# Two of six up parts regular, the input's sums in one later job, maxima across partitions off GpSimd, the last batch's sums on TensorE

## The chip, the cores and the metric

One core of one Trainium2 chip runs the whole program. The metric is the device time of one execution in microseconds, as a median over runs. TensorE (PE), VectorE (DVE), ScalarE (ACT) and GpSimd (POOL) each work through a queue of their own in program order; SyncE (SP) issues the DMAs. An instruction that waits holds up everything behind it on its engine.

## The reference

Batch 4, sequence 448, model width 768, hidden width 3072, all fp32 (the weights of the two later stages arrive as fp64 bits).

```python
attn = 1 / (1 + exp(-(q @ k.T / 8 - log(448))))        # 12 heads of 64
x = concat_heads(attn @ v)                             # 4 x 448 x 768
u = x + real(fft(fft(x, axis=1), axis=2))
un = (u - mean(u)) / sqrt(var(u) + 1e-6)               # over the 768 features
x2 = u + relu(un @ w_ch1) @ w_ch2                      # 768 -> 3072 -> 768
gate = sigmoid(causal_conv5(x2, conv_w))
out = (gate * (x2 @ w_val)) @ w_out
```

## The kernel before, in words

**Order of the work.** The program is written by a planner at build time: jobs are Python generators on a board, and a model of the engines' times decides in which order their instructions are written. At run time only that order and the waits on data count.

**Stages.** First attention (64-row fp32 matmuls), batch by batch, with the Fourier transforms and the layer norm of earlier batches in between. Then the hidden layer in six parts `g` of 512 columns. A part is an *up* product (`un @ w1[g]`, relu, split into two fp16 halves `h`) for all four batches, and a *down* product (`h @ w2[g]`, added into `acc` by VectorE). Each fp32 product is three fp16 matmuls: high by high, high by low, low by high. A down product of one part is 288 matmuls of 128x448. Last come `value` (`wv`) and `project` (`wo`) with the gate.

**Two kinds of up.** `up` is the regular one: 288 matmuls a part. `quad` is a Strassen scheme over a pair of batches, the two halves of the 768 features and two column blocks: seven products instead of eight, 252 matmuls a part. For it the weights are combined (seven blocks in `load_w1`, with adds on VectorE) and the inputs too: `sums(pair)` makes sums and differences `tb` of `un` on GpSimd, with fp16 roundings on ScalarE, 72 GpSimd instructions for both pairs, and overwrites half of the second batch's `un`. The seven results are put together on VectorE and ScalarE in `combine`. Before, part 0 is regular and parts 1 to 5 are Strassen.

**Weights.** Every weight goes through `convert`: 384 columns at a time are loaded as 64-bit words, turned into fp32 by integer instructions (five on VectorE, one on ScalarE), and their largest magnitude is kept. The first three (`w1[0]`, `w2[0]`, `w1[1]`) go into SBUF; the other 13 matrices (`w2[1]`, `w1[2]`, `w2[2]`, and so on to `wo`) go by `stream` back to DRAM and are read again later (`again`) into the one buffer `wf`, since their scale is known only when the whole matrix has been seen. `factor` makes the scale from the largest magnitude over all partitions. For the early three it goes by `peak`: VectorE writes a diagonal `pd`, TensorE multiplies it with ones, VectorE takes the maximum of each row. For the 13 of the stream it goes by `peak_pool`, a `partition_all_reduce` on GpSimd. `load_w2` scales a down weight in four quarters on ScalarE (`wf`, then the fp16 high half `w`) and makes the low half on GpSimd (for part 0 on VectorE).

**Sums of the norm.** `norm(b)` adds up six tiles of features on VectorE or GpSimd, then one fp32 matmul with ones adds over partitions; for the variance the squares are added in the same way before four small fp32 matmuls.

In the profile all engine instructions carry one line (L218, the recorder of the planner), so they are told apart by the names of their tiles.

Of the kernel before, what the change touches and what calls it, by code (L numbers as in the profile page):

```python
# [8 lines left out]
F32 = mybir.dt.float32  # L9
F32R = mybir.dt.float32r  # L10
F16 = mybir.dt.float16
# [40 lines left out]
S_BY = "DVE"  # L52
NABS = 3
H_BY = "POOL"
T_BY = "POOL", "POOL"
# [6 lines left out]
ABSMAX = bass.bass_isa.ReduceOp.absmax  # L62
# [3 lines left out]
class Clock:  # L66
# [4 lines left out]
    def __init__(self):  # L71
        self.at = dict(PE=0.0, DVE=0.0, ACT=0.0, POOL=0.0, SP=0.0)
        self.cells, self.slots, self.spans, self.bytes = {}, {}, {}, {}
        self.port, self.dma, self.log, self.mode = (0.0, ""), 0.0, [], None
# [69 lines left out]
    def put(self, e, cost, reads, writes, lag=0.06, shared=False, tag=None):  # L144
        need = max([self.ready(e, *reads)] + [self.free(e, a) for a in writes])
        start = max(self.at[e], need)
        if shared and start < self.port[0] and self.port[1] != e:
            cost += 0.8 * min(cost, self.port[0] - start)
        end = start + cost
        if shared:  # L150
            self.port = (end, e)
        self.log.append((e, tag, self.at[e], start, end))
        self.at[e] = end
        self.touch(e, reads, writes, end + lag)
        return end

    def note(self, e, op, a, k):
# [24 lines left out]
        if op == "partition_all_reduce":  # L182
            k = dict(out=a[0], in_=a[1])
# [10 lines left out]
        elif e == "POOL":  # L194
            cost = 1.03 if k.get("op") == ALU.pow else 0.41 if op == "partition_all_reduce" else 0.12 + n * (0.002 if out.dtype == F16 else 0.00224)
# [54 lines left out]
def when(go):  # L250
    return (), (), 0, go
# [89 lines left out]
def body(tc, qd, kd, vd, w1d, w2d, cwd, wvd, wod, cdd, k12d, csd, eyed, out):  # L341
# [83 lines left out]
    def peak_pool(m, nm):  # L425
        yield on("DVE", m)
        t = col(nm + "t")
        V.tensor_reduce(out=t, in_=m, axis=AX.X, op=ALU.max)
        yield on("POOL", t)
        g = col(nm + "g")  # L430
        P.partition_all_reduce(g, t, 128, ABSMAX)
        then = ck.at["POOL"] + 4.0
        yield when(lambda: board.by(then))
        return g

# [82 lines left out]
    def first_f32(src, i, exp, nm):  # L518
# [3 lines left out]
        yield from factor(m, W1N, i, exp, nm, True)  # L522
# [5 lines left out]
    def stream():  # L528
# [3 lines left out]
        for i in range(2):  # L532
            jobs += [(wvd[i], ("wv", i), 12 + i, WV_EXP), (wod[i], ("wo", i), 14 + i, WO_EXP)]
# [15 lines left out]
        def scaling():  # L549
            for j, (last, n, key, i, exp, d) in enumerate(ends):  # L550
                yield when(lambda: done[0] >= last)
                yield from factor(mx[:, j % 2], n, i, exp, key[0], False)
# [36 lines left out]
    def load_w1(g, now=None):  # L589
        if g == 0:  # L590
            t, e, s = yield from first_f32(w1d[0], 0, W1_EXP, "w1")
            w = wp.tile([128, 2 * W1N + 128], F16, tag="w1", bufs=1, name="w1")[:, :2 * W1N].rearrange("p (c n) -> p c n", c=2)
            yield from halves_direct(t, s, w[:, 0], w[:, 1])
            w1_of[0] = w[:, 0].rearrange("p (c k f) -> p c k f", c=8, k=3), w[:, 1].rearrange("p (c k f) -> p c k f", c=8, k=3), e
# [4 lines left out]
        yield when(lambda: g - 1 in upped and len(seen) >= 4 * (g - 1) and w1p.at is not None)  # L599
# [8 lines left out]
        his, lows = [], []  # L608

        def low():  # L610
            for i in range(7):
# [11 lines left out]
        for k, c, o, a, b, need in ((0, 0, None, 0, 0, None), (2, 3, None, 0, 0, None), (1, 1, None, 0, 0, None), (3, 3, ALU.add, 2, 3, 2), (5, 2, ALU.subtract, 0, 2, 2), (4, 0, ALU.subtract, 3, 0, 0), (6, 1, ALU.subtract, 1, 0, 1)):  # L623
# [7 lines left out]
        yield when(lambda: len(lows) == 7)  # L631

    def load_w2(g):
# [7 lines left out]
        yield from (halves_direct if g == 0 else halves_scaled)(t, s, w[:, 0], w[:, 1])  # L641
# [28 lines left out]
    def weights(second):  # L670
# [3 lines left out]
        for nm in ("wv", "wo"):  # L674
            for i in range(2):
                yield from load_half(i, nm)
                if (nm, i) == ("wv", 0):
                    yield when(lambda: ("wo", 1) in kept)
# [4 lines left out]
                    for h in range(2):  # L683
# [3 lines left out]
                        r = col(f"evo{h}")  # L687
                        V.tensor_tensor(out=r, in0=em, in1=factors[:, 0, 14 + h:15 + h], op=ALU.mult)
                        evo.append(r)
# [327 lines left out]
    def norm(b):  # L1017
# [5 lines left out]
        e = yield on(SUM_BY, x[:, 0:2], cost=0.6)  # L1023
        ENG[e].tensor_tensor(out=t, in0=x[:, 0], in1=x[:, 1], op=ALU.add)
        e = yield on(SUM_BY, x[:, 2], t, cost=0.6)
        ENG[e].tensor_tensor(out=t, in0=t, in1=x[:, 2], op=ALU.add)
        yield when(lambda: b in mixed)
        for j in (3, 4, 5):
            e = yield on(SUM_BY, t, x[:, j])
            ENG[e].tensor_tensor(out=t, in0=t, in1=x[:, j], op=ALU.add)  # L1030
        yield on("PE", t, go=banks(1))
        mean = ps_m()
        T.matmul(mean[:, :S], ones, t, start=True, stop=True)
# [22 lines left out]
        yield when(lambda: "s0" in sqs)  # L1056
        e = yield on(SUM_BY, tt[:, 0:2])
        ENG[e].tensor_tensor(out=tt[:, 1], in0=tt[:, 1], in1=tt[:, 0], op=ALU.add)
        yield when(lambda: "s1" in sqs)
        e = yield on(SUM_BY, tt[:, 2:4])  # L1060
        ENG[e].tensor_tensor(out=tt[:, 3], in0=tt[:, 3], in1=tt[:, 2], op=ALU.add)
        e = yield on(SUM_BY, tt[:, 1], tt[:, 3])
        ENG[e].tensor_tensor(out=tt[:, 3], in0=tt[:, 3], in1=tt[:, 1], op=ALU.add)
        sqs.append("a")
        yield when(lambda: "s2" in sqs)
        e = yield on(SUM_BY, tt[:, 0:2])
        ENG[e].tensor_tensor(out=tt[:, 1], in0=tt[:, 1], in1=tt[:, 0], op=ALU.add)
        e = yield on(SUM_BY, tt[:, 1], tt[:, 3])
        ENG[e].tensor_tensor(out=tt[:, 1], in0=tt[:, 1], in1=tt[:, 3], op=ALU.add)
        t = tt[:, 1]  # L1070
        yield on("PE", t, go=banks(1))
        var = ps_m()
        for i in range(4):
            T.matmul(var[:CK, i:i + 1], t[:, i * CK:(i + 1) * CK], ones[:, 0:1], start=True, stop=True)
# [44 lines left out]
    def sums(pair):  # L1119
        b, c = 2 * pair, 2 * pair + 1  # L1120
        yield when(lambda: c in normed and ux.at is not None and (pair == 0 or pair - 1 in tb))
        yield when(lambda: ("up", c) in upped)
        w = ux.tile([128, 3, 2, 3, S], F16, name=f"tb{pair}")
        tmp = ux.tile([128, 3, S], F32, tag="tmp", bufs=1, name="tmp")
        x, y, z = (tmp[:, i] for i in range(3))

        def two(out, p, q, op):
            e = yield on(T_BY[pair], p, q)
# [7 lines left out]
        for k in range(3):  # L1136
            yield from two(x, un_hi[b][:, k], un_lo[b][:, k], ALU.add)
            yield from two(y, un_hi[c][:, k], un_lo[c][:, k], ALU.add)
            yield from two(z, un_hi[c][:, k + 3], un_lo[c][:, k + 3], ALU.add)
            yield from two(x, y, x, ALU.subtract)  # L1140
            yield from two(y, z, y, ALU.subtract)
            yield from part(x, w[:, 0, 0, k], w[:, 0, 1, k])
            yield from two(z, z, x, ALU.subtract)
            yield from part(y, un_hi[c][:, k], un_lo[c][:, k])
            yield from part(z, w[:, 1, 0, k], w[:, 1, 1, k])
            yield from two(x, un_hi[b][:, k + 3], un_lo[b][:, k + 3], ALU.add)
            yield from two(x, x, z, ALU.subtract)
            yield from part(x, w[:, 2, 0, k], w[:, 2, 1, k])
        low, high = slice(0, 3), slice(3, 6)
        tb[pair] = [(un_hi[b][:, low], un_lo[b][:, low]), (un_hi[b][:, high], un_lo[b][:, high]), (un_hi[c][:, high], un_lo[c][:, high])]  # L1150
        tb[pair] += [(w[:, 2, 0], w[:, 2, 1]), (w[:, 0, 0], w[:, 0, 1]), (w[:, 1, 0], w[:, 1, 1]), (un_hi[c][:, low], un_lo[c][:, low])]
# [11 lines left out]
    for pair in range(2):  # L1163
        board.add(T_RANK, sums(pair))
# [35 lines left out]
    SLOT = (0, 2), (3, 1)  # L1200

    def up(b):
        pair, o = divmod(b, 2)
        w1h, w1l, _ = w1_of[0]
        for q in range(2):
# [4 lines left out]
            for i in range(2):  # L1210
                m = 0
                for k in range(NT):
                    c = 4 * (i ^ o) + 2 * (k // 3) + q
                    pump()
                    for w, u in ((w1h, un_hi[b]), (w1h, un_lo[b]), (w1l, un_hi[b])):
                        T.matmul(p[:, i, :S], w[:, c, k % 3], u[:, k], start=(m == 0), stop=(m == 17))
# [3 lines left out]
        upped.add(("up", b))  # L1220
# [159 lines left out]
    ups, downs = list(range(B)), list(range(B))  # L1380
    force(lambda: 0 in w1_of)
    while downs:
        if ups:
            can_down = 0 in w2_of and downs[0] not in ups
            force(lambda: ups[0] in normed or 0 in w2_of and downs[0] not in ups)
            if ups[0] in normed:
                up(ups.pop(0))
                if not ups:
                    upped.add(0)
                continue  # L1390
        force(lambda: 0 in w2_of)
        down(0, downs.pop(0))
    downed.add(0)
# [29 lines left out]
    def value(b, j):  # L1423
        force(lambda: b in xs_of and ("wv", j // 3) in halves)
# [19 lines left out]
    def project(b, j):  # L1444
        force(lambda: ("wo", j // 3) in halves)
# [120 lines left out]
```

## Time and profile before

| | us |
|---|---|
| median of 3 runs | 1063.74 (1062.57 to 1064.6) |
| the profiled execution | 1060.32 |
| its span, first to last instruction | 1058.5 |
| TensorE busy in the span | 995.3 (94%) |
| VectorE busy | 796.2 (75%) |
| ScalarE busy | 490.3 (46%) |
| GpSimd busy | 317.0 (30%) |

Busy times of TensorE count matmuls that overlap; how much the stage needs is better read from the distance between starts. The page's 40 slices show TensorE at 9 tenths or more nearly everywhere; slices 14 to 16 (344 to 423 us) show 5 tenths, and there its granted clock falls to 8, 8 and 7 tenths.

### The profile page before, as it was taken

To read this page: it belongs to the slowest core of one execution; us is meant where nothing else is said; L and a number is where in the kernel's file an instruction comes from. 1 tells how busy PE (TensorE), PEld (TensorE's weight loads), DVE (VectorE), ACT (ScalarE), POOL (GpSimd) and SP (SyncE) were. 2 spreads that over 40 slices of the span, in tenths; PEclk is the share of its full clock that TensorE was granted. 3 is DMA by queue.
4 is the path that set the end of the run, shared out by engine and by line. 5 is a ranking of instruction groups with operands and counts; after the bars stand their busy time and mean duration, and the time that the engine had idled before them with its cause. 6 is when DMAs were issued, how large, how long until landed. Compare 5 with 4: busy or idle time off the path is not lost.

```text
span 1058.5 us, 15662 instructions
## 1 busy us (share of the span) xinstructions
PE 995.3 (94%) x5913; PEld 514.4 (49%) x5913; DVE 796.2 (75%) x1498; ACT 490.3 (46%) x691; POOL 317.0 (30%) x231
## 2 busy tenths in 40 slices
PE   9899999999989555999999989997999999999998
PEld 4344544664545222555555545543555555555554
DVE  4868988879999944887989879957983477776530
ACT  6786756243244344234623452433433588434321
POOL 0104333327959832013302330033113565000000
PEclk9999999999999887999999999999999999999999
DMA  7752340010222443276435544643441021010001
GB/s 235 215 164 82 118 142 1 3 40 22 62 67 90 134 149 115 73 233 198 143 127 178 173 135 150 180 149 109 132 157 46 1 90 46 1 44 36 28 34 70
DMA packets 54547, 110.29 MB, mean 104 GB/s; under 512 B 6456, under 2 KB 30408, under 8 KB 54472
## 3 DMA queue, kind: packets, MB, share of 16 engines
q1 hardware_dynamic: 54472, 109.30, 32.3%
q8 instruction: 46, 0.75, 0.3%
q14 instruction: 29, 0.24, 0.1%
HBM read 84.76 MB, written 24.38 MB: 103 GB/s over the span
## 4 chain that ended last, share of the span: by engine, by line
PE 72%; DVE 17%; issue 6%; ACT 2%; POOL 2%; DMA 1%; SPq 0%; DVEq 0%; POOLq 0%; ACTq 0%
PE ps_m L218 58%; PE ps_s L218 14%; DVE wabs L218 6%; DVE wf L218 3%; DVE c L218 2%; DVE acc L218 1%; DVE tt L218 1%; DVE pm L218 1%; POOL tt L218 1%; POOL w L218 1%; DMA w<-wod 1%; POOL h L218 1%; ACT c L218 0%; DMA v<-vd 0%; SPq L218 0%
## 5 line engine op out<-in xcount | busy, mean ns | idle before, releaser
L218 PE MATMUL ps_m<-h,w 128*128 128x448 f16 x1728 | 332.9, 355 | 14.2 <-POOL w L218 10.2
L218 PEld LDWEIGHTS <-w 128*128 128x128 f16 x2016 | 198.3, 99 | 201.8 <-issue 11.0
L218 ACT ACTIVATE wabs<-w 128x384 f32<-128x384 f32 (+1 forms) x119 | 65.1, 550 | 155.8 <-DMA w<-w2d 44.9
L218 DVE SCALAR_TENSOR_TENSOR wabs<-w,wabs 128x384 int32<-128x384 int32 x192 | 130.7, 681 | 4.7
L218 PEld LDWEIGHTS <-w1hi 128*128 128x128 f16 x840 | 82.9, 99 | 97.7 <-issue 22.0
L218 DVE SCALAR_TENSOR_TENSOR acc<-ps_m,rg,acc 128x448 f32<-128x448 f32 x144 | 97.9, 680 | 38.8 <-PE ps_m L218 36.4
L218 POOL TENSOR_TENSOR h<-c,h 128x896 f16<-128x896 f32 x40 | 77.9, 1952 | 102.5 <-ACT h L218 66.8
L218 ACT ACTIVATE sg<-ps_s,logb 128x896 f32<-128x896 f32 x84 | 83.6, 1004 | 32.1 <-PE ps_s L218 31.2
L218 ACT ACTIVATE c<-c 128x896 f32<-128x896 f32 x40 | 38.0, 950 | 121.6 <-DVE c L218 119.8
L218 PE MATMUL ps_m<-sg,v 64*64 64x448 f32 x672 | 84.1, 548 | 3.6 <-DVE zl L218 2.6
L218 PE MATMUL ps_s<-q,k 64*64 64x448 f32 x672 | 83.5, 543 | 4.2 <-ACT sg L218 4.2
L218 PE MATMUL ps_m<-xs,wv 128*128 128x448 f16 x432 | 84.6, 352 | 0.0
L218 PE MATMUL ps_m<-gh,wo 128*128 128x448 f16 x288 | 80.8, 352 | 0.0
L218 PE MATMUL ps_s<-tb,w1hi 128*128 128x448 f16 x240 | 65.3, 353 | 13.6 <-POOL tb L218 10.7
L218 DVE SCALAR_TENSOR_TENSOR gp<-acc,cw,gp 128x448 f32<-128x448 f32 x84 | 61.4, 731 | 21.8 <-ACT gp L218 19.9
L218 DVE TENSOR_SCALAR_CACHE_REDUCE wabs<-wabs 128x384 f32<-128x384 f32 x120 | 65.3, 544 | 7.4 <-ACT wabs L218 7.1
L218 PE MATMUL ps_s<-un,w1hi 128*128 128x448 f16 x240 | 67.1, 362 | 0.2 <-DVE c L218 0.2
L218 PEld LDWEIGHTS <-w1lo 128*128 128x128 f16 x420 | 41.5, 99 | 51.9 <-issue 14.4
L218 PE MATMUL ps_m<-un,w1hi 128*128 128x448 f16 x240 | 65.0, 352 | 0.0
L218 PEld LDWEIGHTS <-wo 128*128 128x128 f16 x432 | 42.3, 98 | 39.5
L218 PEld LDWEIGHTS <-wv 128*128 128x128 f16 x432 | 42.1, 98 | 39.2
L218 PE MATMUL ps_s<-un,w 128*128 128x448 f16 x288 | 57.7, 360 | 0.0
(170 smaller groups left out, 1512.2 us busy)
## 6 DMA issues: line engine op xcount, KB each, us to landing
w<-w1d SPq DMA_DIRECT2D x48, 384.0 KB
w<-w2d SPq DMA_DIRECT2D x48, 384.0 KB
w<-wabs SPq DMA_DIRECT2D x72, 192.0 KB
wf<-w SPq DMA_DIRECT2D x36, 384.0 KB
q<-qd SPq DMA_DIRECT2D x24, 224.0 KB
out<-o SPq DMA_DIRECT2D x24, 224.0 KB
k<-kd SPq DMA_DIRECT2D x23, 224.0 KB
w<-wvd SPq DMA_DIRECT2D x12, 384.0 KB
```

The costliest lines, as they stand in the source:

```text
L218: return f(*a, **k)
```

## The change

Five edits. (1) `REG = 2`: parts 0 and 1 are regular, 2 to 5 Strassen; `load_w1(1)` makes four blocks and no sums of weights. (2) `sums` is one job for both pairs. It starts when the last batch is normed and `w2[0]` is made, keeps `un` whole, and makes the one operand that overwrites `un` only after the regular part 1 has read it; 84 GpSimd instructions in place of 72. (3) Every maximum across partitions goes by `peak`; `peak_pool` is gone. (4) For the last batch (`BY_PE`) the sums of mean and variance are accumulated by TensorE from the single tiles: 6 fp32 matmuls for 1, and 24 small ones for 4. (5) `w2[0]` is split as the later ones (low half on GpSimd); `wv` and `wo` stream in the order wv, wv, wo, wo; the planner's model of the port that VectorE and GpSimd share is another.

```diff
-T_BY = "POOL", "POOL"
+REG = 2
+START = 0
+T_BY = "POOL"
+BY_PE = (3,)
...
-    def factor(m, n, i, exp, nm, early):
-        g = yield from (peak if early else peak_pool)(m[:, :n // COLS], nm)
+    def factor(m, n, i, exp, nm):
+        g = yield from peak(m[:, :n // COLS], nm)
...
 def load_w1(g, now=None):
-        yield when(lambda: g - 1 in upped and len(seen) >= 4 * (g - 1) and w1p.at is not None)
+        yield when(lambda: g - 1 in upped and len(seen) >= 4 * (g - REG) and w1p.at is not None)
+        num = 4 if g < REG else 7
+        plan = [(0, 0, None, 0, 0, None), (1, 1, None, 0, 0, None), (3, 2, None, 0, 0, None), (2, 3, None, 0, 0, None)]
...
 def load_w2(g):
-        yield from (halves_direct if g == 0 else halves_scaled)(t, s, w[:, 0], w[:, 1])
+        yield from halves_scaled(t, s, w[:, 0], w[:, 1])
...
 def norm(b):
+        if b in BY_PE:
+            mean = ps_m()
+            for j in range(NT):
+                if j == 2:
+                    yield when(lambda: b in mixed)
+                yield on("PE", x[:, j])
+                T.matmul(mean[:, :S], ones, x[:, j], start=(j == 0), stop=(j == NT - 1))
...
+            for k in range(3):
+                yield when(lambda: f"s{k}" in sqs)
+                for h in range(2):
+                    q = tt[:, 2 * k % 4 + h]
+                    for i in range(4):
+                        T.matmul(var[:CK, i:i + 1], q[:, i * CK:(i + 1) * CK], ones[:, 0:1], start=(k + h + i == 0), stop=(k + h + i == 6))
...
-    def sums(pair):
-        yield when(lambda: c in normed and ux.at is not None and (pair == 0 or pair - 1 in tb))
-        yield when(lambda: ("up", c) in upped)
+    def sums():
+        yield when(lambda: B - 1 in normed and START in w2_of)
+        for w, b, c in zip(ws_, (0, 2), (1, 3)):
+            for k in range(3):
+                yield from two(x, un_hi[b][:, k], un_lo[b][:, k], ALU.add)
...
+        for w, b, c in zip(ws_, (0, 2), (1, 3)):
+            yield when(lambda: ("up", REG - 1, c) in upped)
+            for k in range(3):
+                v, y = tmp[:, k % 2], tmp[:, 2]
+                yield from two(v, un_hi[c][:, k + 3], un_hi[c][:, k], ALU.subtract)
+                yield from two(y, un_lo[c][:, k + 3], un_lo[c][:, k], ALU.subtract)
+                yield from two(v, v, y, ALU.add)
+                yield from part(v, un_hi[c][:, k], un_lo[c][:, k])
...
-    for g in range(1, NG):
+    for g in range(REG, NG):
         for pair in range(2):
             force(lambda: pair in tb and g in made)
             for q in range(2):
                 quad(g, pair, q, c)
```

GpSimd's queue before, while part 1 goes from its Strassen up to its down product (`tb` and `tmp` are the input's sums, `h` the hidden layer's low halves, `w_3623` the low half of `w2[1]`, and an ISA row with no tile stands on either side of each maximum):

```order
L218 TENSOR_TENSOR tmp<-tmp 128x448
L218 ISA
L218 ISA w2g<-w2t 128x1
L218 ISA
L218 TENSOR_TENSOR tb_3131<-tmp,tb_3131 128x448
L218 TENSOR_TENSOR h<-c,h 128x896
L218 TENSOR_TENSOR w_3623<-wf,w_3623 128x768
L218 TENSOR_TENSOR h<-c,h 128x896
L218 TENSOR_TENSOR w_3623<-wf,w_3623 128x768 x2
L218 ISA
L218 ISA w1g<-w1t 128x1
L218 ISA
```

The same queue of the changed kernel, at the same weight (`w_3693` is now the low half of `w2[1]`):

```order
L219 TENSOR_TENSOR un<-tmp,un 128x448
L219 TENSOR_TENSOR w_3693<-wf,w_3693 128x768 x2
L219 TENSOR_TENSOR tmp<-un 128x448
L219 TENSOR_TENSOR w_3693<-wf,w_3693 128x768 x2
L219 TENSOR_TENSOR tmp<-un 128x448
L219 TENSOR_TENSOR tmp<-tmp 128x448
L219 TENSOR_TENSOR un<-tmp,un 128x448
```

The maxima and their ISA rows are gone, and all `tb` rows stand earlier; what follows the low half is only the last operand, which overwrites `un`.

ScalarE's queue of the changed kernel at the end of the regular up of part 1 (`h<-ps_s` is the relu of one block, the last of eight is the lower one; `wf` and `w_3693` are the quarters of `w2[1]`):

```order
L219 ACTIVATE h<-ps_s 128x2x448
L219 ACTIVATE wabs<-w_3666 128x384
L219 ACTIVATE wf<-wf,factors 128x768
L219 ACTIVATE w_3693<-wf 128x768
L219 ACTIVATE wf<-wf,factors 128x768
L219 ACTIVATE w_3693<-wf 128x768
L219 ACTIVATE h<-ps_s 128x2x448
L219 ACTIVATE wf<-wf,factors 128x768
L219 ACTIVATE w_3693<-wf 128x768
L219 ACTIVATE wf<-wf,factors 128x768
L219 ACTIVATE w_3693<-wf 128x768
```

Two of the four quarters stand behind the relu of the last block of the up product, which waits for TensorE; there is no such place in the kernel before.

TensorE's queue of the changed kernel at the norm of the last batch, in pieces (`ps_s<-un,w` is the regular up of part 0, LDWEIGHTS its weight loads):

```order
L219 MATMUL ps_m<-acc_104,ones 128x448 x6
L219 LDWEIGHTS w_770
L219 MATMUL ps_s<-un,w_770 128x448
...
L219 MATMUL ps_m<-pd,ones_r 128x128
...
L219 MATMUL ps_m<-ones,tt 112x1 x24
```

Before, these were one matmul `ps_m<-tt,ones 128x448` and four `ps_m<-ones,tt 112x1`; the `pd` row is the maximum of `w2[0]`, which stood further up. From here to the end the queue has 13 `pd` rows more than before, one for each matrix of the stream.

## Rows read from the trace of the kernel before

**Rows 1.** Waits of TensorE: waiter <- releaser: us in total, times, longest us.
```profile
PE ps_s L218 <- POOL tb L218: 10.7, 1, 10.7
...
PE ps_m L218 <- POOL w L218: 10.2, 1, 10.2
...
PE ps_m L218 <- ACT tb L218: 10.0, 1, 10.0
...
PE ps_m L218 <- DVE pd L218: 3.9, 2, 3.3
```

**Rows 2.** Timeline of TensorE: start us, busy us, instructions merged, [idle before <-releaser].
```profile
325.93 0.54 PE L218 MATMUL ps_m<-un,w1hi 128*128 128x448 f16 x2
...
412.83 55.01 PE L218 MATMUL ps_m<-h,w 128*128 128x448 f16 x277 [10.21 <-POOL w L218]
...
515.35 54.64 PE L218 MATMUL ps_m<-h,w 128*128 128x448 f16 x288
...
630.07 10.22 PE L218 MATMUL ps_m<-h,w 128*128 128x448 f16 x46 [3.33 <-DVE acc L218]
...
734.20 26.08 PE L218 MATMUL ps_m<-h,w 128*128 128x448 f16 x137
...
836.35 24.00 PE L218 MATMUL ps_m<-h,w 128*128 128x448 f16 x126
```

**Rows 3.** Timeline of GpSimd around three maxima across partitions, same columns.
```profile
374.44 0.41 POOL L218 PARTITION_ALL_REDUCE w2g<-w2t  x1 [5.66 <-issue]
...
382.98 1.02 POOL L218 TENSOR_TENSOR tb<-tmp,tb 128x448 f16<-128x448 f32 x1 [8.13 <-ACT w L218]
...
402.17 0.41 POOL L218 PARTITION_ALL_REDUCE w1g<-w1t  x1 [5.90 <-DVE wabs L218]
...
409.31 1.87 POOL L218 TENSOR_TENSOR h<-c,h 128x896 f16<-128x896 f32 x1 [6.73 <-issue]
...
411.15 1.62 POOL L218 TENSOR_TENSOR w<-wf,w 128x768 f16<-128x768 f32 x1
...
619.11 3.72 POOL L218 TENSOR_TENSOR h<-c,h 128x896 f16<-128x896 f32 x2 [7.89 <-issue]
```

**Rows 4.** Windows: each engine busy us (xcount) in a stretch; then PE clock, DMA.
```profile
340.00:412.00 72.00, 39.98 (x190) 19.15 (x188) 47.04 (x84) 30.74 (x45) 38.88 (x29) 0.80 0.38 121
...
515.00:617.00 102.00, 102.00 (x541) 52.78 (x540) 91.15 (x185) 43.69 (x62) 21.03 (x13) 1.00 0.52 165
```

**Rows 5.** Timeline of VectorE: a maximum across partitions by way of TensorE.
```profile
294.03 0.15 DVE L218 TENSOR_REDUCE w1t<-wm 128x1 f32<-128x8 f32 x1
...
294.92 0.29 DVE L218 TENSOR_REDUCE w1g<-ps_m 128x1 f32<-128x128 f32 x1 [0.42 <-PE ps_m L218]
```

**Rows 6.** Timeline of TensorE: fp32 sums of the last batch, and that maximum.
```profile
241.64 0.99 PE L218 MATMUL ps_m<-tt,ones 128*128 128x448 f32 x2 [1.29 <-DVE tt L218]
...
242.47 7.54 PE L218 MATMUL ps_s<-un,w 128*128 128x448 f16 x39
...
253.82 0.86 PE L218 MATMUL ps_m<-ones,tt 128*112 128x1 f32 x8
...
294.56 0.33 PE L218 MATMUL ps_m<-pd,ones_r 128*128 128x128 f32 x1 [3.27 <-DVE pd L218]
```

**Rows 7.** Timeline of ScalarE: a hidden block, then one quarter of a down weight.
```profile
298.89 0.92 ACT L218 ACTIVATE h<-ps_s 128x896 f16<-128x896 f32 x1 [3.37 <-PE ps_s L218]
...
380.81 0.92 ACT L218 ACTIVATE wf<-wf,factors 128x768 f32<-128x768 f32 x1
...
381.76 0.84 ACT L218 ACTIVATE w<-wf 128x768 f16<-128x768 f32 x1
```

**Rows 8.** Timeline of VectorE: the same two instructions of the weight stream, twice.
```profile
360.19 2.67 DVE L218 SCALAR_TENSOR_TENSOR wabs<-w,wabs 128x384 int32<-128x384 int32 x2
...
379.84 1.15 DVE L218 SCALAR_TENSOR_TENSOR wabs<-w,wabs 128x384 int32<-128x384 int32 x2
```

**Rows 9.** Groups by line on GpSimd: xcount, busy us, mean ns, idle before.
```profile
L218 POOL TENSOR_TENSOR tmp<-tmp 128x448 f32<-128x448 f32 x24 | 32.2, 1342 | 0.9
```

More of the change, by code (lines that the diff above doesn't have):

```diff
@@ L146, in put @@
         start = max(self.at[e], need)
-        if shared and start < self.port[0] and self.port[1] != e:
-            cost += 0.8 * min(cost, self.port[0] - start)
         end = start + cost
         if shared:
-            self.port = (end, e)
+            other = self.port["POOL" if e == "DVE" else "DVE"]
+            if other > start:
+                end = max(end, other + cost - 0.14)
+            self.port[e] = end
         self.log.append((e, tag, self.at[e], start, end))
@@ L194, in note @@
         elif e == "POOL":
-            cost = 1.03 if k.get("op") == ALU.pow else 0.41 if op == "partition_all_reduce" else 0.12 + n * (0.002 if out.dtype == F16 else 0.00224)
+            cost = 1.03 if k.get("op") == ALU.pow else 0.12 + n * (0.002 if out.dtype == F16 else 0.00224)
             shared = op == "tensor_tensor"
@@ L1022, in norm @@
         yield when(lambda: (b, 2) in added)
[L1023 to L1033, printed above, removed]
+        if b in BY_PE:
+            yield on("PE", x[:, 0:2], go=banks(1))
+            mean = ps_m()
[4 more added lines that the diff above has]
+                T.matmul(mean[:, :S], ones, x[:, j], start=(j == 0), stop=(j == NT - 1))
+        else:
+            e = yield on(SUM_BY, x[:, 0:2], cost=0.6)
+            ENG[e].tensor_tensor(out=t, in0=x[:, 0], in1=x[:, 1], op=ALU.add)
+            e = yield on(SUM_BY, x[:, 2], t, cost=0.6)
+            ENG[e].tensor_tensor(out=t, in0=t, in1=x[:, 2], op=ALU.add)
+            yield when(lambda: b in mixed)
+            for j in (3, 4, 5):
+                e = yield on(SUM_BY, t, x[:, j])
+                ENG[e].tensor_tensor(out=t, in0=t, in1=x[:, j], op=ALU.add)
+            yield on("PE", t, go=banks(1))
+            mean = ps_m()
+            T.matmul(mean[:, :S], ones, t, start=True, stop=True)
         yield when(lambda: len(homes) > b)
@@ L1134, in part @@
             yield from two(l, f, h, ALU.subtract)
[L1136 to L1148, printed above, removed]
@@ L1162, in body @@
         board.add(1, norm(b))
-    for pair in range(2):
-        board.add(T_RANK, sums(pair))
+    board.add(T_RANK, sums())
     scores(0)
@@ L1378, in gate_ends @@
             gps[0, j] = g
[L1380 to L1393, printed above, removed]
+    for g in range(REG):
+        ups, downs = list(range(B)), list(range(B))
+        force(lambda: g in made)
+        while downs:
+            if ups:
+                force(lambda: ups[0] in normed or g in w2_of and downs[0] not in ups)
+                if ups[0] in normed:
+                    up(g, ups.pop(0))
+                    if not ups:
+                        upped.add(g)
+                    continue
+            force(lambda: g in w2_of)
+            down(g, downs.pop(0))
+        downed.add(g)
     force(lambda: B - 1 in normed)
     c = u1.tile([128, 4, S], F32, tag="tt", bufs=1, name="c")
-    for g in range(1, NG):
+    for g in range(REG, NG):
         for pair in range(2):
@@ L1423, in value @@
     def value(b, j):
-        force(lambda: b in xs_of and ("wv", j // 3) in halves)
+        force(lambda: b in xs_of and ("wv", j // 3) in halves and len(rv) == 2)
         xh, xl, _ = xs_of[b]
@@ L1444, in project @@
     def project(b, j):
-        force(lambda: ("wo", j // 3) in halves)
+        force(lambda: ("wo", j // 3) in halves and len(evo) == 2)
         if j == 0:
```

128 lines of the change are left out of this document (71 added, 57 removed).

## The prediction

> **What bounds the kernel now.** The page first: TensorE is busy nearly throughout, so a gain can only come from where it isn't, and slices 14 to 16 are that place. The list of TensorE's waits comes next: three waits of 10.7, 10.2 and 10.0 us stand far above the rest [rows 1]. All three wait for GpSimd or for ScalarE's rounding between two GpSimd steps: twice for the input's sums `tb`, once for the low half of a down weight `w`. The window over that place shows TensorE busy for 40 of 72 us while VectorE is busy for 47 and GpSimd for 39 [rows 4], so no engine there is at its limit all the time; something holds up a queue.
>
> The timeline of TensorE gives the price. A stage without a gap is the pair of part 4's down and part 5's up: 540 matmuls from 734.20 to 836.35, 0.1892 us each [rows 2]. Against this rate:
> - from 325.93 (part 1's up begins) to 412.83, 252 + 11 matmuls took 86.9 us and need 49.8: 37.1 lost;
> - from 412.83 to 515.35, 277 + 252 took 102.5 and need 100.1: 2.4 lost behind the wait, where TensorE starts at the lower of its two clocks (the granted clock is 0.80 on average in the window [rows 4]);
> - from 515.35 to 734.20, 1080 took 218.9 and need 204.3: 14.5 lost.
>
> Together 54.0 us. The timeline of GpSimd says what held it up [rows 3]. A maximum across partitions is busy for 0.41 us, but GpSimd stands still for 5.7 to 5.9 us ahead of it and does its next work 8.1, 6.7 and 7.9 us after it, two of these with nothing that the profile could name ("issue"). So one costs GpSimd some 14 us, and what is queued behind it waits: the `tb` at 382.98, released into TensorE's 10.7; the `h` at 409.31 and the `w` at 411.15, released into its 10.2; the `h` at 619.11, after which VectorE and TensorE came late (3.3 us at 630.07 [rows 2]). The reader is to see that the row's 0.41 us is not the price; the distance to the neighbours is.
>
> **The change part by part.**
>
> *Maxima off GpSimd.* All 13 go, and their 13 holes of 14 us. In their place VectorE and TensorE do what they do for the early weights: from 294.03 to 294.92 + 0.29 [rows 5] it is 1.2 us from the maximum in each partition to the one over all. On TensorE each `pd` is one more matmul; 13 at the rate of 0.19 are **+2.5 us**. If each takes its whole 0.33 [rows 6], it is 4.3. On VectorE it is 0.29 for the second maximum and 0.32 for the diagonal (from 294.18 to 294.92 less the wait of 0.42), 8 us in all, beside a stage that holds TensorE full with VectorE busy for 91 of 102 us [rows 4]; that cover is thin.
> The Trainium skill (GPSIMD Engine Reference, section 4.1, Engine selection) speaks against this edit: it puts a reduction along the partitions on GpSimd. By the rows here it is 1.2 us against 14 [rows 3, 5]; by the rule the edit gains nothing, 10.7 + 10.2 + 14.5 of the losses above stay, and the sum below would end at 1062.
>
> *Sums in one job.* 84 instructions at 1.34 us [rows 9] are 113 us of GpSimd, 16 more than before. But they are due at part 2's up and no longer at part 1's: two products of 288, 109 us, later. 60 of them can run from the norm of the last batch on; of the other 24, 12 wait for the end of part 1's up, so 16 us of them, and 4 x 1.62 of down weights [rows 3], lie inside a down product of 54.6 us [rows 2]. So nothing is due before it can be done, and the 10.0 and 10.7 go. I take the whole 37.1 + 2.4 + 14.5 as gone: **-54.0 us**. The lower bound is what doesn't hang on a maximum or on `tb`: if the 14.5 stays, since VectorE is late for another reason, it is -39.5.
>
> *Part 1 regular.* 36 more matmuls at 0.1892: **+6.8 us** on TensorE. VectorE and ScalarE lose four `combine` and seven weight sums and blocks, and get eight `h`; this lies beside it.
>
> *The down weight of part 1.* This is a new wait. Two quarters of `w2[1]` stand in ScalarE's queue behind the relu of the last block of the up product, which can only begin when TensorE ends that product (time T). Then 0.92 for the relu, 0.92 + 0.84 for a quarter [rows 7], 1.62 for its low half [rows 3]: the third quarter is ready at T + 4.3, the fourth at T + 6.1. TensorE's first tile takes 12 matmuls (2.3 us), three to a quarter; with the last three it ends at T + 6.7. **+4.4 us**. Behind 3.33 us of waiting, 46 matmuls took 10.22 in place of 8.7 [rows 2]: a low clock could add 1.5. The other end is nothing, if ScalarE is ahead of the order as I read it; it can't be ahead of TensorE, so I take 4.4.
>
> *Sums of the last norm on TensorE.* 5 more fp32 matmuls at 0.83 (241.64 to 242.47 [rows 6]) are 4.2; 20 more small ones, at 0.86 for four, are 4.3. They take the place of a sum on VectorE for which TensorE waited 1.3, and of 3.3 us at a `pd` that VectorE brought late [rows 6], while VectorE loses those sums and the low halves of `w2[0]`. 8.5 - 1.3 - 3.3 is **+3.9**; if the late `pd` stays, +7.2. The work that fills the norm's latency is now the rest of the regular up, and 72 + 30 matmuls of it stand behind the last matmul of the norm.
>
> *The rest.* The order wv, wv, wo, wo and the other port model move instructions in stretches where TensorE is full; at nothing, with TensorE's queue as the cover. If the cover fails, it is the second rival below.
>
> Sum: 1060.3 - 54.0 + 2.5 + 6.8 + 4.4 + 3.9 = 1023.9 for an execution like the profiled one. The median of the runs stands 3.4 above that one's time (1063.74 against 1060.32), so 1027.
>
> **The rivals.**
>
> *VectorE becomes the bound.* With the holes gone the same stream must pass in less time. Two instructions of it take 1.15 us alone and 2.67 while GpSimd works beside them [rows 8], and the sums still run beside the streams of `w1[1]` and `w2[1]`. For: VectorE at 91 of 102 us. Against: in that very stretch TensorE lost nothing [rows 4], and part 1 takes work off VectorE. If the 16 pieces of these two weights each cost 1.5 us more and half of that reaches TensorE, it is 12; with the 1.5 of the low clock, 1041. Up to 1052 if all of it does.
>
> *Every `pd` is waited for.* It stands in TensorE's queue, and where VectorE is late, all matmuls behind it wait; the one of [rows 6] cost 3.3 us. 13 times that is 43, and 1023.9 + 3.4 + 43 is 1070: slower than before. From 2.8 us each on (36.6 over 13), the whole gain is gone. For it speaks that row; against it, the kernel before has 11 such matmuls and only two of them were waited for, 3.9 us together [rows 1]. This is also how the skill's rule above would come out right.
>
> *The waits are not the maxima's.* GpSimd's holes could be its own way of waiting for ScalarE's data, and stay with the low halves. Then the change only pays for its 36 matmuls and more where it doesn't shift `tb`: about 1063, no change. Against it: 6.7 and 7.9 us that the profile gives to nobody, behind maxima [rows 3].
>
> *More than that.* ScalarE and VectorE come in time for `w2[1]`, and the norm has no wait: 1027 - 4.4 - 4 and some of the early waits, 1008 to 1016.
>
> **How the numbers follow.** Forecast 1016 to 1040: 0.62. VectorE the bound, 1040 to 1054: 0.17. More gain, 1008 to 1016: 0.13. Every `pd` waited for: 0.05. Holes stay: 0.03. The range that leaves out no more than 2 in 10 takes the forecast and half of both neighbours: 1011 to 1046. A difference of under 0.2% (2 us) can't be told from none here. Faster is 0.62 + 0.17 + 0.13 = 0.92, same 0.03, slower 0.05.
>
> **What would show it.** The maxima right: no idle of 6 to 8 us "issue" on GpSimd, and no wait of TensorE for `h` or `tb`. The sums right: part 2's up begins without a wait for `tb`. Part 1: TensorE busy without a gap for 54.5 us, then some 4 us of waiting for ScalarE's or GpSimd's `w` at the start of its down product. The norm: 6 fp32 matmuls in 5 us, and no gap over 2 us up to the next up. The prediction is wrong if TensorE's list shows waits for `pd` or for VectorE above 15 us in total, or if the stretch from part 1's up to part 5's still loses more than 20 us against 0.1892 a matmul.

## The result and the profile after

| | before | after |
|---|---|---|
| median | 1063.15 us (4 runs, 1059.87 to 1064.6) | 1031.28 us (4 runs, 1029.61 to 1035.43) |
| the profiled execution | 1060.32 | 1032.49 |
| its span | 1058.5 | 1030.4 |

The ratio of the mean times is 0.971, with a 95% interval of 0.9672 to 0.9749: faster, by about 32 us. The forecast was 1027, its own range 1016 to 1040.

The page of the changed kernel, its first part (busy us, share, instructions) and two rows of the 40 slices:

```profile
PE 1006.5 (98%) x6012; PEld 525.3 (51%) x6012; DVE 806.6 (78%) x1499; ACT 484.0 (47%) x681; POOL 296.9 (29%) x217
...
PE   9899999999999999999999999989999999999998
...
PEclk9999999998999999999999999999999999999999
```

The hole of slices 14 to 16 is gone, and so is the low granted clock there. One slice of the granted clock is left at 8, the one from 232 to 258 us, and it is new: the norm of the last batch, below.

TensorE's list of waits (waiter, releaser, us in total, times, longest):

```profile
PE ps_m L219 <- DVE pd L219: 8.6, 8, 2.6
...
PE ps_m L219 <- POOL w L219: 3.2, 3, 1.5
...
PE ps_m L219 <- ACT w L219: 0.5, 1, 0.5
```

The three waits of some 10 us of [rows 1] are gone, and none is for `tb` or `h`. At the top stands `pd`, with 8.6 us in place of 3.9; three of its eight waits make up 5.3 of them (2.63 and 2.15 in parts 4 and 5, 0.56 just ahead of the last stage). Where the time went is best seen in a table of stages, each from the start of an up product to the next one's, read from the timeline of TensorE:

| stage | before, us | after, us |
|---|---|---|
| up to part 1's up | 325.9 | 329.1 |
| part 1 | 141.8 | 115.3 |
| part 2 | 102.2 | 102.6 |
| part 3 | 107.0 | 102.8 |
| part 4 | 111.9 | 106.0 |
| part 5 | 102.6 | 107.5 |
| value and project, to the end | 167.2 | 167.2 |

Part 1 has 36 matmuls more than before (6.8 us) and still is 26.5 us shorter. Parts 3 and 4 give 10 us. Part 5 and the stretch ahead of part 1 are longer than before: there the change costs something.

Part 1's down product, on the timeline of TensorE (start, busy, operation, idle before and its releaser):

```profile
383.61 1.11 PE L219 MATMUL ps_m<-h,w 128*128 128x448 f16 x5
385.57 0.36 PE L219 MATMUL ps_m<-h,w 128*128 128x448 f16 x1 [0.86 <-POOL w L219]
386.48 0.55 PE L219 MATMUL ps_m<-h,w 128*128 128x448 f16 x2 [0.54 <-ACT w L219]
388.48 0.74 PE L219 MATMUL ps_m<-h,w 128*128 128x448 f16 x3 [1.45 <-POOL w L219]
390.08 2.19 PE L219 MATMUL ps_m<-h,w 128*128 128x448 f16 x6 [0.86 <-POOL w L219]
```

The regular up of part 1 ran from 329.05 to 383.61 without a gap: 54.6 us for 288 matmuls and one `pd`, as forecast. Then come four waits of 3.7 us in sum: the first for the low half of the second quarter of `w2[1]`, which GpSimd ended only at 385.51, the others for the third and fourth quarter. The 88 matmuls behind the last of them took 18.2 us in place of 16.6, at the lower clock at first.

GpSimd's timeline at the same place:

```profile
371.64 1.04 POOL L219 TENSOR_TENSOR un<-tmp,un 128x448 f16<-128x448 f32 x1 [1.71 <-ACT un L219]
381.95 3.56 POOL L219 TENSOR_TENSOR w<-wf,w 128x768 f16<-128x768 f32 x2 [9.27 <-ACT w L219]
```

The longest idle time there, 9.27 us, waits for ScalarE's data (`w`); idle times "issue" of 6 to 8 us, as in [rows 3], are in no row of its groups any more.

The norm of the last batch, on the timeline of TensorE, and the window around it (its length, busy us and instructions of PE, PEld, DVE, ACT, POOL; granted clock, DMA share, GB/s):

```profile
229.86 4.67 PE L219 MATMUL ps_m<-acc,ones 128*128 128x448 f32 x12
...
237.85 6.89 PE L219 MATMUL ps_m<-ones,tt 128*112 128x1 f32 x48
244.60 8.69 PE L219 MATMUL ps_s<-un,w 128*128 128x448 f16 x30
```

```profile
229.00:256.00 27.00, 27.00 (x135) 17.30 (x134) 20.01 (x31) 11.81 (x14) 7.40 (x5) 0.81 0.15 45
```

Six fp32 sums take 4.5 us (229.86 to 234.37). The 24 narrow matmuls, one column each, take 6.75 us (237.85 to 244.60), where four of them took 0.72 before [rows 6]. In that window the granted clock is 0.81 on average, and the 30 matmuls behind take 8.5 us in place of 5.7. How long the clock stays low here differs between executions. Three kernels of the experiments have the same order on TensorE up to this place, and in theirs the 24 take 4.7 to 5.0 us and the window's clock is 0.94. Here are the row and the window of the one with the maxima back on GpSimd:

```profile
240.34 4.79 PE L222 MATMUL ps_m<-ones,tt 128*112 128x1 f32 x48
```

```profile
229.00:256.00 27.00, 26.56 (x156) 17.29 (x155) 21.86 (x36) 11.65 (x14) 7.41 (x5) 0.94 0.15 45
```

Last, the longest wait for `pd` of part 5, on the timelines of TensorE, VectorE and GpSimd:

```profile
775.65 0.33 PE L219 MATMUL ps_m<-pd,ones_r 128*128 128x128 f32 x1 [2.15 <-DVE pd L219]
...
776.71 0.95 PE L219 MATMUL ps_s<-un,w1hi 128*128 128x448 f16 x2
```

```profile
773.83 1.76 DVE L219 TENSOR_SCALAR pd<-eye,wot 128x128 fp32r<-128x128 f32 x1
775.51 0.61 DVE L219 TENSOR_TENSOR c<-ps_m,w1lo 128x448 f32<-128x448 f32 x1
```

```profile
773.63 1.88 POOL L219 TENSOR_TENSOR h<-c,h 128x896 f16<-128x896 f32 x1 [1.30 <-ACT h L219]
```

The diagonal of the other long wait, in part 4, on the timelines of VectorE and TensorE:

```profile
681.76 0.63 DVE L219 TENSOR_TENSOR c<-ps_m,w1lo 128x448 f32<-128x448 f32 x1 [2.49 <-issue]
...
685.27 0.29 DVE L219 TENSOR_SCALAR pd<-eye,w2t 128x128 fp32r<-128x128 f32 x1
```

```profile
685.61 0.33 PE L219 MATMUL ps_m<-pd,ones_r 128*128 128x128 f32 x1 [2.63 <-DVE pd L219]
```

In part 4 it took 0.29 us, with no GpSimd instruction beside it; in part 5 it took 1.76 and ended at 775.59. GpSimd's instruction began 0.2 us before it and ended at 775.51. So in part 5 VectorE was held until GpSimd was done (only 0.08 of the diagonal's own 0.29 us lie behind that), TensorE waited 2.15 us for `pd`, and the next matmuls ran at the lower of the two clocks (two of them busy for 0.95 us, against 0.54 in [rows 2]). The Trainium skill says the same of the mechanism (SBUF — State Buffer, section "SBUF: two separate sides"): the port pair that VectorE and GpSimd share is, for the instructions that need it, an exclusive lock for a whole instruction, not a split of bandwidth. The trace agrees, with those two ends 0.08 us apart. The longer wait, 2.63 us in part 4, is not of that kind: VectorE had stood idle for 2.49 us before 681.76, with no releaser that the profile names. The tile `w1lo` that it reads there was written by ScalarE until 681.67, which points to ScalarE; it was not tested.

### The profile page after: what moved, and what is told of

The parts are those of the page before. It is cut to its first block, busy times and chain, and to the rows that moved or that the text cites. A ratio compares the mean times of both kernels' runs of the same rounds, so it can differ in the third digit from the quotient of the medians.

```text
span 1030.4 us, 15792 instructions
## 1 busy us (share of the span) xinstructions
PE 1006.5 (98%) x6012; PEld 525.3 (51%) x6012; DVE 806.6 (78%) x1499; ACT 484.0 (47%) x681; POOL 296.9 (29%) x217
## 5 line engine op out<-in xcount | busy, mean ns | idle before, releaser
L219 DVE SCALAR_TENSOR_TENSOR wabs<-w,wabs 128x384 int32<-128x384 int32 x192 | 142.6, 743 | 4.7
L219 ACT ACTIVATE wabs<-w 128x384 f32<-128x384 f32 x120 | 65.2, 549 | 143.6 <-DMA w<-w2d 56.5
L219 PE MATMUL ps_s<-un,w1hi 128*128 128x448 f16 x384 | 104.6, 354 | 0.0
L219 POOL TENSOR_TENSOR w<-wf,w 128x768 f16<-128x768 f32 x24 | 40.7, 1709 | 209.2 <-ACT w L219 208.9
L219 ACT ACTIVATE sg<-ps_s,logb 128x896 f32<-128x896 f32 x84 | 84.0, 1006 | 31.7 <-PE ps_s L219 30.7
L219 POOL TENSOR_TENSOR h<-c,h 128x896 f16<-128x896 f32 x32 | 62.2, 1943 | 118.7 <-ACT h L219 75.7
L219 PE MATMUL ps_s<-un,w1lo 128*128 128x448 f16 x192 | 68.1, 355 | 0.0
L219 ACT ACTIVATE c<-c 128x896 f32<-128x896 f32 x32 | 30.4, 951 | 76.8 <-DVE c L219 76.8
L219 ACT ACTIVATE wf<-wf,factors 128x768 f32<-128x768 f32 (+1 forms) x60 | 52.3, 881 | 16.1 <-DVE factors L219 8.4
```

The costliest lines, as they stand in the source:

```text
L219: return f(*a, **k)
```

## The experiments

The theory behind the forecast: a maximum across partitions costs GpSimd a standstill of some 14 us, and what is queued behind it waits; the sums' later place keeps the rest of GpSimd's work out of the path. The first rival: the sums came too late, and the maxima only stood near. The second: VectorE is the engine that everything hangs on, through the `pd` rows in TensorE's queue. Times are medians with the 95% interval of the ratio to the kernel before.

**Maxima alone** (the kernel before, one line):

```diff
-        g = yield from (peak if early else peak_pool)(m[:, :n // COLS], nm)
+        g = yield from peak(m[:, :n // COLS], nm)
```

> The kernel before with one edit: the 13 maxima of the stream go by VectorE and TensorE; sums, parts and norm stay as they were. Theory (a maximum across partitions costs GpSimd a standstill of some 14 us, and what is queued behind it waits): the waits of 10.7, 10.0 and 10.2 us at the input's sums and the down weight shrink to under 10 us in sum, the 14.5 us of parts 3 and 4 shrink to a few, 13 more matmuls cost 2.6 to 4: 1018 to 1035 us. Rival (the sums come too late because they are due at part 1's up, and the maxima only happen to stand near): the 10.7 and 10.0 stay, only the down weight's 10.2 may go: 1048 to 1062 us.

Measured: 1047.57 us (0.9833 to 0.9885), between the two theories' ranges and next to the rival's. The list of waits says why:

```profile
PE ps_m L218 <- DVE pd L218: 30.7, 9, 10.2
...
PE ps_s L218 <- POOL tb L218: 1.8, 1, 1.8
```

The waits for `tb` fell from 20.7 us [rows 1] to 1.8, and that for `w` is gone: the first rival is out, for the sums stayed where they were. But TensorE now waits 30.7 us for `pd`, 10.2 at the longest, where it waited 3.9. On VectorE's timeline, just before that longest one:

```profile
347.27 3.43 DVE L218 SCALAR_TENSOR_TENSOR wabs<-w,wabs 128x384 int32<-128x384 int32 x2
...
361.25 1.96 DVE L218 SCALAR_TENSOR_TENSOR wabs<-w,wabs 128x384 int32<-128x384 int32 x2
363.13 0.15 DVE L218 TENSOR_REDUCE w2t<-mx 128x1 f32<-128x8 f32 x1
363.32 1.72 DVE L218 TENSOR_SCALAR pd<-eye,w2t 128x128 fp32r<-128x128 f32 x1
```

The pair of instructions that takes 1.15 us alone [rows 8] takes 3.43 and 1.96 here, and the diagonal 1.72, while GpSimd makes the sums. The waits that were GpSimd's came back as VectorE's: of the 32 us that the same kernel gains once the `pd` stand later (below), half is lost to them.

**Maxima back on GpSimd** (the changed kernel, `peak_pool` put back for the stream, the reverse of the diff above):

> The changed kernel with the 13 maxima of the stream back on GpSimd, all else as changed. Theory of the standstill: GpSimd has idle time to hide most of them, but the one of w2[1] falls between the sums and the low halves that part 1's down product waits for, and others ahead of the hidden layer's low halves: 5 to 25 us more than the changed kernel, 1036 to 1056 us, with idle times of 6 to 8 us behind each maximum. Rival (the sums' later place is what brings the gain): within 3 us of 1031, or less, since the 13 matmuls and 7.7 us at late pd rows go: 1021 to 1034.

Measured: 1056.64 us (0.9913 to 0.9961), 25 us above the changed kernel, just above the first theory's range. One chain, on GpSimd, VectorE and TensorE:

```profile
467.25 0.41 POOL L222 PARTITION_ALL_REDUCE w2g<-w2t  x1 [5.83 <-DVE wabs L222]
477.20 1.87 POOL L222 TENSOR_TENSOR h<-c,h 128x896 f16<-128x896 f32 x1 [9.54 <-issue]
```

```profile
479.10 1.09 DVE L222 TENSOR_TENSOR c<-ps_s,w1lo 128x896 f32<-128x896 f32 x1 [10.49 <-POOL h L222]
```

```profile
480.91 0.84 PE L222 MATMUL ps_s<-un,w1hi 128*128 128x448 f16 x2 [4.80 <-DVE c L222]
```

The maximum starts after 5.8 us of idle time, the next `h` after another 9.5. That `h` reads `c`, so VectorE can't write the next block of `c` and stands for 10.5 us, and TensorE for 4.8. In all, TensorE waits 11.5 us for `c` and 10.8 for `acc` here. The loss is not where it was before the change: no `tb` is waited for, and part 1 takes only 2.8 us more than in the changed kernel; part 2 takes 8.3 more, part 5 10.6 and the last stages 4.8. The later place of the sums took away one victim of the standstill, not the standstill.

**Each maximum twice** (the kernel before):

```diff
         P.partition_all_reduce(g, t, 128, ABSMAX)
+        P.partition_all_reduce(g, t, 128, ABSMAX)
```

> The kernel before with each of the 13 maxima on GpSimd done twice in a row. If the standstill is the price of going to this instruction and back, a second one behind the first costs its own 0.4 us, with no idle of 6 us between the two, and hardly shows: 1063 to 1068 us. If each one costs its 14 us, those in the path add up: the three waits of 10 us double, 1080 to 1110.

Measured: 1068.3 us, one execution (a second one took 2108 us, which stays unexplained, and is left out). GpSimd's timeline:

```profile
379.83 0.87 POOL L218 PARTITION_ALL_REDUCE w2g<-w2t  x2 [6.39 <-issue]
387.48 1.02 POOL L218 TENSOR_TENSOR tb<-tmp,tb 128x448 f16<-128x448 f32 x1 [6.79 <-DVE wabs L218]
...
407.29 0.93 POOL L218 PARTITION_ALL_REDUCE w1g<-w1t  x2 [5.97 <-DVE wabs L218]
414.93 1.87 POOL L218 TENSOR_TENSOR h<-c,h 128x896 f16<-128x896 f32 x1 [6.71 <-issue]
```

Two in a row take 0.87 to 0.93 us, with one idle time before the pair and one behind it. The price is that of going from `TENSOR_TENSOR` to this operation and back, 13.2 us around the first pair and 12.7 around the second, not that of the maximum.

**One regular part** (the changed kernel):

```diff
-REG = 2
+REG = 1
```

> The changed kernel with one regular part, as before, but with the sums in one job: they are due at part 1's up. 36 matmuls (6.8 us) and the waits at part 1's down product (5.2 us) go. In the changed kernel the last sums that the first pair needs end at 372.7 us, and part 1's up begins at 329: if the sums' due time matters, TensorE waits some 35 us for un or tb there: 1045 to 1060. If they would come in time without the maxima's standstill: 1017 to 1024.

Measured: 1060.97 us (0.996 to 1.0001), just above the first range. TensorE's waits:

```profile
PE ps_m L219 <- DVE pd L219: 34.0, 9, 28.5
PE ps_s L219 <- ACT un L219: 12.4, 2, 10.9
```

The 12.4 us for `un` are the sums, too late as expected. The larger wait came from elsewhere: the `pd` of `w2[1]` stands ahead of part 1's up in this order, and VectorE, which shares its port with the sums on GpSimd, came to it 28.5 us late. So the second regular part pays for its 6.8 us: it gives the sums, and VectorE beside them, 54.6 us more.

**The planner's model of the port.** The prediction put this edit at nothing. Twice it was taken alone; the work is the same, only the order in the queues differs. First the changed kernel with the old model:

```diff
-            other = self.port["POOL" if e == "DVE" else "DVE"]
-            if other > start:
-                end = max(end, other + cost - 0.14)
-            self.port[e] = end
+            self.port = (end, e)
...
+        if shared and start < self.port[0] and self.port[1] != e:
+            cost += 0.8 * min(cost, self.port[0] - start)
```

> The changed kernel, planned with the old model of the port that VectorE and GpSimd share; the work is the same, only the order in the queues differs. The prediction put this edit at nothing. If that holds: 1028 to 1035 us. Rival: with the old model VectorE is planned too early, so pd rows stand too early in TensorE's queue, as in before_peak, where TensorE waited 26 us for them: 1040 to 1055, with waits for pd of 15 us or more.

> The kernel before with the stream's maxima on VectorE and TensorE (as before_peak, 1047.6 us) and planned with the new model of the port. If the model is what keeps pd from being waited for in the changed kernel, the 26 us of before_peak fall under 10: 1025 to 1035 us. If it is the sums' later place that does (VectorE works beside a GpSimd that is free of sums), they stay: 1043 to 1052.

The old model in the changed kernel: 1047.64 us (0.9814 to 0.9872), 16 us slower than the new one. The new model in the kernel before with its maxima on VectorE: 1039.84 us (0.9743 to 0.9797), 8 us faster. Their waits of TensorE, in this order:

```profile
PE ps_m L218 <- DVE pd L218: 19.4, 10, 3.3
```

```profile
PE ps_m L219 <- DVE pd L219: 9.9, 10, 2.6
PE ps_m L219 <- ACT w L219: 8.3, 1, 8.3
PE ps_m L219 <- DVE tt L219: 5.5, 2, 3.2
```

The wait for `pd` is 19.4 us with the old model against 8.6 in the changed kernel, and 9.9 with the new one against 30.7 in the run with the maxima alone. So the model does to the waits what the rival said, in both kernels. In the second the time lies between the two expectations, since waits for the halves of `w2[1]` (8.3 us) and for the norm's `tt` (5.5) turn up. Of the 13.4 us between the spans of the first (1043.8 against 1030.4), 5.5 lie behind the start of part 1's up and 7.9 ahead of it; what makes the latter was not taken apart.

**The place of `pd` in TensorE's queue** (12 maxima of the stream in the changed kernel by 4 us of the planner's time; all 13 by 8 us in the kernel before with its maxima on VectorE):

```diff
+        if slack:
+            then = ck.at["DVE"] + slack
+            yield when(lambda: board.by(then))
         yield on("PE", d, go=banks(1))
         p = ps_m()
         T.matmul(p[:, :128], ones_r, d, start=True, stop=True)
```

> The changed kernel, with the matmul of each of the last 12 maxima of the stream written 4 us (in the planner's time) later into TensorE's queue; w2[1]'s stays where it was. If the waits for pd are what the prediction's sum lacked (0.23, 0.43, 2.63 and 2.15 us from part 3 on, and 1.7 us at the lower clock behind the longest two), they go below 1 us in sum: 1023 to 1027 us. If VectorE is late for another reason, the waits only move to its next result (acc or c): 1030 to 1034.

> The kernel before with its stream's maxima on VectorE and TensorE, as in the run before_peak (1047.6 us), and the matmul of each written 8 us later into TensorE's queue. In before_peak TensorE waited 26 us for pd in the stream, 10.2 at the longest. If only the place in the queue is to blame, all but some 4 us of it and the low clock behind go: 1016 to 1026, and then the maxima alone give as much as the whole change. If VectorE itself is behind, the waits turn up at acc or c: 1036 to 1047.

The changed kernel: 1022.13 us (0.9593 to 0.964), 9 us better and better than expected. The other: 1031.81 us (0.9662 to 0.9728), 16 better than the maxima alone, and the same as the whole change, though short of what the theory expected. Of the 9.2 us between the spans of the changed kernel and the first (1030.4 against 1021.2), 2.6 lie ahead of part 1's up (329.05 against 326.41), where the order on all engines is the same and the clock at the norm stayed low for less long. So some 6.5 are the edit's, and 1024.8 would lie inside the range that was expected. Their waits, in this order:

```profile
PE ps_m L219 <- DVE pd L219: 4.2, 5, 1.2
```

```profile
PE ps_m L218 <- DVE pd L218: 17.8, 4, 10.3
...
PE ps_s L218 <- POOL tb L218: 1.9, 1, 1.9
```

In the first, what is left lies in the attention, the early weights and part 5; parts 1 to 4 have no wait for `pd` at all, part 5 has 1.6 us (under 1 was expected from part 3 on), and none moved to `acc` or `c`: the matmul was only written too early. In the second the longest wait stayed (10.3 us at 364.4). The input's sums are where they were before the change there, and TensorE waits 1.9 us for `tb` in all: that the waits for `tb` go does not need the sums in one later job. Why the slack did nothing there was not tested; by the code the planner lets no slack stand while it is pressed for a job that the next product needs.

**The last batch's sums back on VectorE**, both (`BY_PE = ()`) or those of the variance alone:

```diff
-        if b in BY_PE:
+        if False:
             yield on("PE", tt[:, 0:2], go=banks(1))
             var = ps_m()
```

> The changed kernel with the last batch's sums of mean and variance back on VectorE and GpSimd. By the trace of the changed kernel the sums on TensorE cost 4.5 us (6 matmuls), 6.75 us (24 narrow ones) and 2.8 us at the lower clock behind them, against 0.8 + 0.7 us and some 2 us of waits: 1020 to 1025 us if the waits stay as small as before. By the prediction's term it is 3.9 us: 1027. Rival (VectorE is full there, 69.5 of 75 us, so the sums come late and the norm's end is waited for): 1029 to 1036.

> The changed kernel with only the variance's sums of the last batch back on VectorE and GpSimd; the mean stays on TensorE. If the 24 narrow matmuls are what costs (6.75 us against 0.72 us for four, and the granted clock falls behind them, 2.8 us), 8 us go: 1022 to 1026 us, and the matmuls behind the variance run at 0.19 us. Rival (the clock falls because TensorE waits or runs fp32, not because of the narrow ones): the low stretch stays, and no more than 6 us go. Rival (VectorE late): 1029 to 1034.

Both: 1036.45 us (0.972 to 0.9769), no gain: the expectation of 1020 to 1025 missed. The variance alone: 1026.82 us (0.9639 to 0.9688), a gain of 4.5, a little less than expected. TensorE's timeline of the first, a window of the second (columns as above):

```profile
254.72 1.15 PE L219 MATMUL ps_m<-tt,ones 112*128 112x112 f32 x8 [2.32 <-DVE tt L219]
...
264.63 7.71 PE L219 MATMUL ps_m<-h,w 128*128 128x448 f16 x26 [1.96 <-POOL w L219]
```

```profile
229.00:256.00 27.00, 26.50 (x142) 15.21 (x142) 22.74 (x41) 14.20 (x18) 8.64 (x6) 1.00 0.15 45
```

In the first TensorE waits 2.3 us for `tt` and then for the quarters of `w2[0]`: from the last Fourier matmul to part 1's up it takes 98.6 us, where the changed kernel takes 99.8, so the late sums eat up the gain, as the rival said. They do not explain that the kernel is slower. In its profiled execution that stretch begins 6.0 us later (235.27 against 229.28), although up to there all four engines have the same order as in the changed kernel; why is open. With the variance alone moved the granted clock stays at its full level over the same 27 us. So it needs the narrow matmuls to lower it: the fp32 sums are in both. Whether the narrow ones do it without those six fp32 sums ahead of them, no run shows. Part 1's up begins 7.3 us earlier than in the changed kernel (321.77 against 329.05), but part 1 then takes 120.1 us in place of 115.3, since `w2[1]` does not come earlier by as much:

```profile
PE ps_m L219 <- ACT w L219: 3.6, 1, 3.6
PE ps_m L219 <- POOL w L219: 3.1, 4, 1.5
```

6.7 us of waits in place of 3.7, and a low clock behind them: 4.8 of the 7.3 us are given back one stage later.

**Both corrections** (variance on VectorE, `pd` later):

> The changed kernel with both corrections: the last batch's variance summed on VectorE and GpSimd (1026.8 us alone), and the matmul of the stream's last 12 maxima written 4 us later into TensorE's queue (1022.1 alone). The variance on VectorE had already brought the waits for pd from part 3 on from 6.0 to 4.4 us, so the two share a part: if they add up otherwise, 1017 to 1020 us, with waits for pd in parts 2 to 5 under 1.5 us. If the 24 narrow matmuls and the late pd are one and the same loss (VectorE's lateness), no better than 1022.

Measured: 1020.83 us (0.9576 to 0.9615), just above the expected range and the best of all, 10 us below the changed kernel; the waits for `pd` in parts 2 to 5 are 0.8 us, as expected. From the later `pd` alone it can't be told apart by the intervals. TensorE's waits:

```profile
PE ps_m L219 <- ACT w L219: 3.6, 1, 3.6
PE ps_m L219 <- POOL w L219: 3.4, 4, 1.8
PE ps_m L219 <- DVE pd L219: 2.9, 4, 1.2
```

## Why the prediction was right, and where its sum was off

The sum gave 1023.9 for an execution like the profiled one; the profiled one took 1032.5. Point by point:

- **Maxima off GpSimd and the sums in one job, -54.0.** All that was to go went: no wait for `tb` or `h`, the 10.2 us at the down weight gone. Of the 14.5 of parts 3 and 4 some 4.5 stayed, but they belong to `pd` rows: 3.3 of waits (0.23, 0.43 and 2.63, below) and the rows themselves. The mechanism is shown from three sides: by the waits that go when the maxima alone go, by those that come when they alone come back, and by the pair of maxima that costs no more than one. Of the two edits in this term it is the maxima that count: with the sums where they were, the waits for `tb` and `w` went as well.
- **Part 1 regular, +6.8, and 13 `pd`, +2.5.** 54.6 us for the up, forecast 54.5. A `pd` that isn't waited for takes 0.22 us, 2.9 in all.
- **The down weight of part 1, +4.4 and perhaps 1.5.** 3.7 of waits and 1.5 of low clock. The last pieces of the third and fourth quarter came 4.8 and 6.4 us after T, where 4.3 and 6.1 were forecast; the wait for the second quarter's low half was not reckoned with.
- **The norm on TensorE, +3.9.** Mis-sized for the profiled execution. From the last Fourier matmul to part 1's up (229.28 to 329.05), 441 matmuls of the products need 83.4 of 99.8 us; before, 429 needed 81.2 of 91.4 (234.50 to 325.93). So the norm cost 16.3 in place of 10.3: +6. The late `pd` of [rows 6] did shrink from 3.3 to 0.9, but the 24 narrow matmuls took 6.75, where the term had 4.3 for 20 of them and 0.86 for four, and the low clock behind them, 2.8 us, was in no term. The size of it is in part the execution's: in the runs with `pd` later and with the maxima back, with the same order there, the norm cost 14.1 and 13.7 us, some 3.6 more than before, which is the forecast. The stretch ahead of the norm was some 3 us shorter than before, which the sum had at nothing either. It can't be counted on: with the same order it took 6.0 us longer in the run with both sums on VectorE.
- **"The rest, at nothing, with TensorE's queue as the cover."** This is the step that failed. Late `pd` rows from part 3 on cost 6.0 us of waits, and the low clock behind one of them (the 2.15) another 1.7: 7.7 us that the sum lacked. It is the second rival in small: not 3.3 us at each, but 2.6 and 2.2 at two and little at three more. And the edit of the port model, put at nothing, is worth 16 us: without it TensorE waits 19.4 us for `pd` in all, and the kernel takes 1048; only part of that lies at the `pd` rows, as said above. The other two pieces of that edit, the split of `w2[0]` and the order wv, wv, wo, wo, were not taken alone.

The errors (7.7 late `pd`, 2 at the norm with its clock, 1 in part 1, against 3 ahead of the norm) add up to some 8 of the 8.6 us between 1023.9 and 1032.5. The 3.4 that were added for the median were not there after the change: the profiled execution lay 1.2 above its median. The prediction's own signs of being wrong stayed away, if not by far: TensorE's waits for `pd` and VectorE come to 12.8 us (15 was the limit), and from part 1's up to part 5's 11.2 us are lost (20 was the limit).

Of the rivals, "VectorE becomes the bound" and "every `pd` is waited for" turned out to be one: VectorE is late, often beside GpSimd, and TensorE meets that at `pd`. With the maxima alone moved it costs half of the gain, and with the `pd` written later there the kernel reaches 1031.81 us, as fast as the whole change. The changed kernel with later `pd` takes 1022.13, so all the other edits together are worth some 10 us at that point, and one wait for `pd` of 10.3 us that stayed in the run of 1031.81 is as long as that. What the second regular part, the sums in one job and the norm on TensorE bring singly is not shown. The Trainium skill's rule (GPSIMD Engine Reference, section 4.1, Engine selection), by which a reduction along the partitions belongs on GpSimd, does not hold for these small maxima: 25 us slower in the changed kernel, 15 in the one before.

## What to carry to other kernels

A short instruction can have a long price: look at the distance to its neighbours on the engine, and test it by doing it twice. When work is moved off an engine that stands still, look for where it meets the next queue: the place of twelve small matmuls in TensorE's queue was worth some 6.5 us here, a fifth of the change. And an order that a planner's model makes is part of the change and needs a term of its own, even when no instruction differs.

## What the runs showed of the hardware that was not expected

- GpSimd's standstill comes on both sides of a run of maxima: in the rows shown 5.7 to 6.4 us ahead of it and 6.7 to 9.5 behind it until the next `TENSOR_TENSOR`, whether one or two maxima stand between.
- 24 matmuls of one column, behind six fp32 ones, took 4.7 to 6.8 us in four kernels with the same order there, and the granted clock fell to its lower level within or behind them in each: the mean of the window around them was 0.81 in the changed kernel and 0.94 in the three others. With four of them it stayed at 1.00 (variance on VectorE).
- A 128x128 diagonal on VectorE takes 0.29 us alone and took 1.72 and 1.76 in two places beside a GpSimd instruction, ending less than 0.1 us behind it.
